# Low parts of x a group earlier, the router's small matmuls in idle bank pairs, one scaling per group

## The chip, the core and the metric

One core of a Trainium2 chip runs the whole program. The metric is the device time of one execution in microseconds (us); less is better. Five engines work side by side, each through its own instructions in order: TensorE (PE; its weight loads are PEld), VectorE (DVE), ScalarE (ACT), GpSimd (POOL) and SyncE (SP), which here issues the DMAs. SBUF is the on-chip memory, PSUM the memory that TensorE writes its sums into: eight banks, `bank[:, 0..7, :]`.

## What is computed

```python
# attention: p packs k, v into 32 rows per head; q attends to the packed rows   -> x (2304, 512)
h = x @ w_in;  x = (h * cos(h)) @ w_out                                         # first layer
logits = x @ w_gate;  P = exp(logits - logits.max())                            # router, 8 experts
for _ in range(8):
    P /= P.sum(1, keepdims=True) + 1e-09
    P /= P.sum(0, keepdims=True) + 1e-09
    P *= N / E
for e in range(E):                                                              # second layer
    out += P[:, e:e + 1] * (np.maximum(x @ w1[e], 0.0) @ w2[e])                  # 512 -> 1024 -> 512
```

Everything is fp32. A matrix that TensorE reads is split into a high part (fp32r) and a low part (the rest), and a product is three matmuls: high x high, high x low, low x high.

## The kernel before

The first part of the program (attention and first layer) is not touched. The diff lies in the second layer and its entry. The second layer has 16 units (an expert's half each) of three blocks of 768 tokens, which makes 48 **steps**. This text numbers them from 0, as the code's `now` does. A product of 2 x 2 blocks is computed with seven multiplications instead of eight, for x times w1 (`g1_mult`, products 0, 6, 1, 5, 4, 3, 2 of x) and for h times w2 (`g2_mult`, products 1, 5, 6, 3, 7, 2, 4 of h). One product is 12 matmuls of 128x384. The w2 products of a step are computed during the next step.

**A step is four groups**, k = 0 to 3. Group 0 has x's products 0 and 6, then h's products 1 and 5; group 1 has 1 and 5, then 6 and 3; group 2 has 4 and 3, then 7 and 2; group 3, half as long, has 2, then 4. So 24 or 12 matmuls stand in each half of a group. `between` is called after the first x product, and further work is recorded around the parts. The order in which the program is written is the order on each engine; nothing rearranges it.

**PSUM pairs.** x's products go into two pairs of banks, X = `two_banks(x)` and Y (banks 0 to 3), which change roles from step to step; h's products go into two pairs out of banks 4 to 7 (chain 0 and chain 1), which also change roles. X of a step is Y of the step before. A group reads them with ScalarE (L787 copy, L790 copy with a minus sign, L797 copy, L772 relu) and VectorE (L791, L805 add into PSUM); L857 (VectorE) adds a finished h product into the output `acc`, and L859 (ScalarE) writes it where it is the first. Line 746 makes the low half of an h operand behind ScalarE's cast of line 741; L812, L817, L821 are sums of h blocks on VectorE and L813 one on GpSimd.

**x.** During the first unit (steps 0 to 2) the 21 x operands are made: `x_sum` (L652, VectorE), `x_high` (L665, ScalarE cast) and `x_low` (L670, VectorE, followed by two DMAs that store the operand to DRAM, L672), into one of four slots. From the second unit on they are loaded back (L682). Before, `x_steps(n)` does one of each in the same place: low of n-2, high of n-1, sum of n, so that the low part of an operand is written three products ahead of its use.

**Router.** `logits` (32-column matmuls, transposes, `lg_sum`) runs through step 0 and `sinkhorn` behind it, as generators that `step_side` advances by one piece at fixed places. `sinkhorn` takes the maximum (`mx`, a transpose, `top`, ones x top, `nmx`), the exp on ScalarE, then eight rounds of row sums (`rs`) and column sums (`cs`, ones x cs, `rc`), and at the end transposes the probabilities to `p_sb` and stores them to `pd` in DRAM. Its small matmuls need a bank: before, that is bank 2(1-x) for the first two and bank 7 for all others; to keep bank 7 free, steps 3, 4 and 5 are **narrow**: chain 1 has only bank 6, its products are done bank by bank (`NARROW`) and each half is added on its own.

**Scaling.** The first expert's output is scaled by its column of P after the fact: `pb_load` broadcasts a block's probabilities from `pd`, and `scale_first` (L894, VectorE) multiplies one of four pieces of a block in `acc`. Before, these are steps 6, 7, 8, with one, one and two pieces in groups 0, 1 and 2. From the second expert on L775 applies the scale to the relu's result.

The other queues: SP issues all these DMAs in program order; `t_make` and `w1_make` prepare the next unit's weights on ScalarE and GpSimd (L242, L243, L246; L710, L711, L714).

## Time and profile before

| What | us |
|---|---|
| Median of three runs | 1847.51 (1846.35 to 1849.91) |
| The profiled execution, its time | 1848.91 |
| The profiled execution, its span | 1846.6 |
| TensorE busy, of that | 1814.5 |
| VectorE busy | 1479.4 |
| ScalarE, GpSimd busy | 828.2, 831.4 |
| Mean granted TensorE clock | 0.997 of full speed |

The span is the time from the first to the last instruction. The granted clock is the share of TensorE's full clock (2.4 GHz) that it was given: 1.00, or 0.50 (1.2 GHz). "Idle before" in a row is the time in which the engine had nothing to run, and the arrow names what ended it. A busy time can be longer than the work: VectorE's passes of 128x768 last about 0.95 us in most rows, and about 2 us in some.

### The profile page before, as it was taken

To read this page: it belongs to the slowest core of one execution; us is meant where nothing else is said; L and a number is where in the kernel's file an instruction comes from. 1 tells how busy PE (TensorE), PEld (TensorE's weight loads), DVE (VectorE), ACT (ScalarE), POOL (GpSimd) and SP (SyncE) were. 2 spreads that over 40 slices of the span, in tenths; PEclk is the share of its full clock that TensorE was granted. 3 is DMA by queue.
4 is the path that set the end of the run, shared out by engine and by line. 5 is a ranking of instruction groups with operands and counts; after the bars stand their busy time and mean duration, and the time that the engine had idled before them with its cause. 6 is when DMAs were issued, how large, how long until landed. Compare 5 with 4: busy or idle time off the path is not lost.

```text
span 1846.6 us, 29714 instructions
## 1 busy us (share of the span) xinstructions
PE 1814.5 (98%) x11751; PEld 1770.5 (96%) x11751; DVE 1479.4 (80%) x1613; ACT 828.2 (45%) x1243; POOL 831.4 (45%) x542
## 2 busy tenths in 40 slices
PE   7999999998999999999999999999999999999998
PEld 4799999988999999999999999999999999999998
DVE  5876877557697998888888888888788888888886
ACT  5877777655644333333333333333333333333333
POOL 3545554554343545454545444444444544544420
PEclk9999999999999999999999999999999999999999
DMA  8511111035657666666766666666666666666652
GB/s 294 182 47 46 47 58 58 1 133 189 220 194 234 224 221 218 229 211 211 229 219 211 213 229 218 211 223 220 235 210 230 222 211 219 212 228 220 212 190 108
DMA packets 220982, 345.58 MB, mean 187 GB/s; under 512 B 13852, under 2 KB 190764, under 8 KB 220844
## 3 DMA queue, kind: packets, MB, share of 16 engines
q1 hardware_dynamic: 220844, 343.68, 56.2%
q8 instruction: 93, 1.52, 0.3%
q14 instruction: 45, 0.37, 0.1%
HBM read 322.32 MB, written 21.31 MB: 186 GB/s over the span
## 4 chain that ended last, share of the span: by engine, by line
PE 89%; DVE 6%; ACT 2%; issue 1%; DMA 1%; POOL 1%; SPq 0%; ACTq 0%; DVEq 0%; POOLq 0%
PE bank L763 35%; PE bank L837 35%; PE bank L606 11%; PE bank L547 2%; PE bank L549 2%; PE bank L548 2%; DVE hreg L746 1%; DVE acc L857 1%; DMA k<-kT 1%; PE bank L483 1%; DMA pb<-pd 0%; DVE slot L746 0%; DVE xl L670 0%; PE bank L899 0%; ACT raw L772 0%
## 5 line engine op out<-in xcount | busy, mean ns | idle before, releaser
L837 PE MATMUL bank<-hreg,thi 128*128 128x384 f32 x2016 | 516.4, 337 | 2.8 <-DVE acc L857 2.0
L763 PE MATMUL bank<-xh 128*128 128x384 f32 x1344 | 454.4, 338 | 4.8 <-DVE top L948 3.4
L763 PE MATMUL bank<-xl,xh 128*128 128x384 f32 x1344 | 452.5, 337 | 1.8 <-DVE xl L670 1.8
L763 PE MATMUL bank<-xh,xl 128*128 128x384 f32 x1344 | 452.3, 336 | 0.0
L857 DVE TENSOR_TENSOR acc<-bank,acc 128x768 f32<-128x768 f32 (+1 forms) x343 | 313.4, 916 | 113.1 <-PE bank L837 110.7
L837 PEld LDWEIGHTS bank<-hreg,thi 128*128 128x128 f32 x2016 | 365.1, 188 | 4.6 <-ACT thi L242 1.3
L746 DVE TENSOR_TENSOR hreg<-raw,hreg 128x768 fp32r<-128x768 f32 x252 | 332.2, 1326 | 22.6 <-ACT hreg L741 22.5
L837 PE MATMUL bank<-hreg,tlo 128*128 128x384 f32 x1008 | 339.3, 337 | 0.0
L741 ACT CAST hreg<-raw 128x768 fp32r<-128x768 f32 x252 | 207.2, 835 | 278.6 <-DVE raw L821 134.5
L243 POOL TENSOR_TENSOR tlo<-raw,thi 128x512 fp32r<-128x512 f32 x112 | 168.0, 1505 | 260.7 <-ACT thi L242 254.9
L813 POOL TENSOR_TENSOR raw<-raw,raw 128x768 f32<-128x768 f32 x48 | 89.3, 1861 | 395.4 <-DVE raw L812 395.4
L763 PEld LDWEIGHTS bank<-xh 128*128 128x128 f32 x1344 | 253.0, 188 | 7.0 <-DVE top L948 3.8
L763 PEld LDWEIGHTS bank<-xl,xh 128*128 128x128 f32 x1344 | 253.5, 189 | 2.4 <-DVE xl L670 2.4
L763 PEld LDWEIGHTS bank<-xh,xl 128*128 128x128 f32 x1344 | 253.2, 188 | 0.0
L711 POOL TENSOR_TENSOR xl<-wraw,xh 128x512 fp32r<-128x512 f32 x112 | 188.5, 1695 | 124.3 <-ACT xh L710 124.3
L837 PEld LDWEIGHTS bank<-hreg,tlo 128*128 128x128 f32 x1008 | 189.3, 188 | 0.0
L606 PE MATMUL bank<-hreg,whi 128*128 128x288 f32 x1024 | 188.1, 296 | 0.2 <-DVE rbuf L587 0.2
L775 DVE SCALAR_TENSOR_TENSOR raw<-bank,pb 128x768 f32<-128x768 f32 x168 | 160.0, 952 | 18.5 <-PE bank L763 13.8
L837 PE MATMUL bank<-slot,thi 128*128 128x384 f32 x672 | 171.6, 336 | 0.6 <-DVE acc L857 0.6
L606 PEld LDWEIGHTS bank<-hreg,whi 128*128 128x128 f32 x1024 | 153.0, 188 | 1.9 <-DVE rbuf L587 1.1
L242 ACT CAST thi<-raw 128x512 fp32r<-128x512 f32 x112 | 68.0, 619 | 157.9 <-POOL raw L246 156.5
L563 POOL TENSOR_TENSOR hreg<-rbuf,hreg 128x576 fp32r<-128x576 f32 x64 | 91.8, 1437 | 96.4 <-ACT hreg L557 86.8
(153 smaller groups left out, 2681.0 us busy)
## 6 DMA issues: line engine op xcount, KB each, us to landing
xh<-xd SPq DMA_DIRECT2D x315, 384.0 KB, 3.4
xl<-xd SPq DMA_DIRECT2D x315, 384.0 KB, 4.1
raw<-w SPq DMA_DIRECT2D x32, 512.0 KB, 6.0
wraw<-w SPq DMA_DIRECT2D x30, 512.0 KB, 6.3
pb<-pd SPq DMA_DIRECT2D x25, 384.0 KB, 5.4
raw<-w_in SPq DMA_DIRECT2D x16, 512.0 KB, 3.8
raw<-w_out SPq DMA_DIRECT2D x16, 512.0 KB, 3.7
xd<-xh SPq DMA_DIRECT2D x21, 384.0 KB, 3.1
```

The source lines that it names most:

```text
L242: nc.scalar.copy(hi, src)
L243: nc.gpsimd.tensor_tensor(out=lo, in0=src, in1=hi.bitcast(F32), op=ALU.subtract)
L563: nc.gpsimd.tensor_tensor(out=lo, in0=r, in1=hi.bitcast(F32), op=ALU.subtract)
L606: nc.tensor.matmul(ps[:, di, 0:HC], lhsT=lhsT, rhs=rhs, start=(n in (0, 6)), stop=(n in (17, 23)),)
L711: nc.gpsimd.tensor_tensor(out=lo, in0=src, in1=hi.bitcast(F32), op=ALU.subtract)
L741: nc.scalar.copy(hi, step_tiles(s)[H_SRC[m]])
L746: nc.vector.tensor_tensor(out=lo, in0=step_tiles(s)[H_SRC[m]], in1=hi.bitcast(F32), op=ALU.subtract)
L763: nc.tensor.matmul(dst, lhsT=w, rhs=t[:, k, :], start=start and k == 0 and w is a and t is th, stop=k == 1 and w is bq, skip_group_check=True,
L775: nc.vector.scalar_tensor_tensor(out=out, in0=src, scalar=0.0, in1=scale, op0=ALU.max, op1=ALU.mult)
L813: nc.gpsimd.tensor_tensor(out=r21, in0=r11, in1=r21, op=ALU.subtract)
L837: nc.tensor.matmul(dst, lhsT=w, rhs=t[:, p, :], start=start and p == 0 and w is a and t is hh, stop=p == 1 and w is bq, skip_group_check=True,
L857: nc.vector.tensor_tensor(out=dst, in0=src, in1=dst, op=ALU.add)
```

## The change

- `x_first` and `x_next` replace `x_steps`. With q the product that a place stands behind, `x_high(q+4)` is written right after that product, and `x_low(q+4)` and `x_sum(q+6)` after the next part: the low part is now written four products ahead of its use, and so is the sum.
- `sinkhorn` yields True where it next needs a bank, and `step_side(b)` goes on there only where a bank is given. It is given in step 0 (bank 7), in group 0 of step 1 (once), and from group 2 of step 2 on at three places of a step: after the first product of group 0 and of group 3 (the first bank of chain 1's pair), and after the first part of group 2 (bank 2-2x, of Y). The pieces in between are cut differently: `rc` and the multiplication that follows are now one piece with the next round's row sums.
- Steps 3 to 5 are no longer narrow.
- `SCALES` puts one piece of the first expert's scaling into a group: block 0 from group 2 of step 5, block 1 from group 3 of step 6, block 2 from group 3 of step 7. The first `pb_load` moves from group 3 to group 0 of step 5, and the other early ones move with it.

```diff
-    free = {}
+    free = {"need": False}
     def sinkhorn():
         nc.vector.tensor_reduce(mx, lg, axis=AX.XY, op=ALU.max)
-        for _ in range(4):
-            yield
-        t_ps = bank[:, free["bank"], :]
+        yield True
+        ps = bank[:, free["bank"], :]
...
+        yield False
+        yield False
+        yield True
+        ps = bank[:, free["bank"], :]
+        nc.tensor.matmul(ps[:, 0:1], lhsT=ones[0:1, :], rhs=top, start=True, stop=True)
...
             nc.vector.tensor_reduce(cs, prob.rearrange("p t e -> p e t"), axis=AX.X, op=ALU.add)
-            yield
-            yield
-            c_ps = bank[:, 7, :]
-            nc.tensor.matmul(c_ps[:, 0:E], lhsT=ones, rhs=cs, start=True, stop=True)
+            yield True
+            ps = bank[:, free["bank"], :]
+            nc.tensor.matmul(ps[:, 0:E], lhsT=ones, rhs=cs, start=True, stop=True)
...
-    def step_side():
+    def step_side(b=None):
         while side:
+            if free["need"] and b is None:
+                return
+            free["bank"] = b
...
-        def x_steps(n, tmp, end=7 * NJ):
-            if 1 < n <= end + 1 and (n > 5 or end == 4):
+        def x_first(n, tmp):
+            if 1 < n:
                 x_low(n - 2)
...
+        SCALES = {
+            divmod(at + n, 4): (i, n) for i, at in enumerate((22, 27, 31)) for n in range(4)
+        }
-                narrow = s in (NJ * U1 + 3, NJ * U1 + 4, NJ * U1 + 5, NJ * NU - 1)
+                narrow = s == NJ * NU - 1
...
+                    def side_at(place):
+                        if now == 0:
+                            step_side(7)
+                        elif now > 2 or now == 2 and k > 1 or (now, k, place) == (1, 0, 1):
+                            step_side({
+                                (0, 1): banks[1][0], (2, 2): 2 - 2 * x, (3, 1): banks[1][0],
+                            }.get((k, place)))
...
-                        if 2 * NJ <= now < 3 * NJ:
-                            for n in ((0,), (1,), (2, 3), ())[k]:
-                                scale_first(now - 2 * NJ, n, pb[(2, 2, 0)[now - 2 * NJ]])
-                        if busy or k == 3:
-                            free["bank"] = 2 * (1 - x)
-                            step_side()
+                        if (now, k) in SCALES:
+                            scale_first(*SCALES[now, k], pb[2 if now < 7 or now == 7 and k < 3 else 0])
+                        side_at(1)
+                        if qs:
+                            x_next(x_high, qs[0] + 4)
...
-                            if first_unit and 2 * k + n < 7 and 7 * j + 2 * k + n + 3 < 7 * NJ + 2:
-                                x_steps(7 * j + 2 * k + n + 5, [halves(t) for t in pb])
+                            side_at(2 + n)
+                            if n == 0 and len(qs) > 1:
+                                x_next(x_high, qs[1] + 4)
+                            if n < len(qs):
+                                x_next(x_low, qs[n] + 4)
+                                x_next(x_sum, qs[n] + 6, tmp)
...
-                        (5, 3, 1, 0, 0), (5, 3, 0, 0, 2), (5, 3, 1, 1, 1), (6, 2, 0, 1, 2),
+                        (5, 0, 0, 0, 2), (5, 2, 1, 0, 0), (5, 2, 1, 1, 1), (6, 1, 0, 1, 2),
```

Three places show what this does to the engines' order. The first is ScalarE at the turn from step 0 to step 1: L772 relu of group 3, then `x_high` (L665), weight and h casts, and group 0's two copies (L787 and L790). Before:

```order
L772 ACTIVATE raw_4410<-bank 128x768
L665 CAST xh<-pb_3998 128x2x384
L242 CAST thi<-raw_4059 128x512
L741 CAST hreg<-raw_4411 128x768
L787 COPY raw_4001<-bank 128x768
L790 ACTIVATE base<-bank 128x768
L859 COPY acc_101<-bank 128x2x384
```

The same place after the change:

```order
L741 CAST hreg<-raw_4411 128x768
L787 COPY raw_4001<-bank 128x768
L955 ACT_TABLE_LOAD
L955 ACTIVATE prob<-lg,nmx 128x144
L665 CAST xh<-pb_3997 128x2x384
L790 ACTIVATE base<-bank 128x768
L859 COPY acc_101<-bank 128x2x384
```

The router's exp with its table load, which stood in step 2's group 3, and a cast of x now stand between the two copies of group 0.

The second is VectorE from there into group 1: L805 of step 0's group 3, low parts (L670) and sums (L652) of x, h splits (L746) and sums (L817, L821), L791 of group 0. Before:

```order
L805 TENSOR_TENSOR bank<-bank,base 128x2x384
L670 TENSOR_TENSOR xl<-acc_101,xh 128x2x384
L746 TENSOR_TENSOR hreg<-raw_4411,hreg 128x768
L817 TENSOR_TENSOR raw_4411<-raw_4411,raw_4408 128x768
L791 TENSOR_TENSOR bank<-bank,raw_4001 128x2x384
L746 TENSOR_TENSOR hreg<-raw_4411,hreg 128x768
L670 TENSOR_TENSOR xl<-pb_3998,xh 128x2x384
L652 TENSOR_TENSOR pb_3998<-acc_101,pb_3998 128x768
L670 TENSOR_TENSOR xl<-pb_3997,xh 128x2x384
L821 TENSOR_TENSOR raw_4411<-raw_4410,raw_4411 128x768
```

After the change, from the pass behind L805 on:

```order
L947 TENSOR_REDUCE top<-bank 1x1
L670 TENSOR_TENSOR xl<-pb_3998,xh 128x2x384
L652 TENSOR_TENSOR pb_3998<-acc_101,pb_3998 128x768
L746 TENSOR_TENSOR hreg<-raw_4411,hreg 128x768
L817 TENSOR_TENSOR raw_4411<-raw_4411,raw_4408 128x768
L954 COPY nmx<-bank 128x1
L791 TENSOR_TENSOR bank<-bank,raw_4001 128x2x384
L746 TENSOR_TENSOR hreg<-raw_4411,hreg 128x768
L670 TENSOR_TENSOR xl<-pb_3997,xh 128x2x384
L670 TENSOR_TENSOR xl<-pb_3998,xh 128x2x384
L652 TENSOR_TENSOR pb_3997<-acc_1628 128x768
L821 TENSOR_TENSOR raw_4411<-raw_4410,raw_4411 128x768
```

`top` and `nmx`, which stood in steps 1 and 2, stand here now, and one more sum of x lies ahead of the first L746.

The third is VectorE in groups 2 and 3 of step 2: two adds L857 and a split L746 before, and L805 of group 3. Before:

```order
L812 TENSOR_TENSOR raw_4411<-raw_4409,raw_4000 128x768
L857 TENSOR_TENSOR acc_101<-bank,acc_101 128x2x384
L746 TENSOR_TENSOR hreg<-raw_4408,hreg 128x768
L857 TENSOR_TENSOR acc_1628<-bank,acc_1628 128x2x384
L805 TENSOR_TENSOR bank<-bank,base 128x2x384
L953 COPY nmx<-bank 128x1
```

After the change, from the first of those adds on:

```order
L857 TENSOR_TENSOR acc_101<-bank,acc_101 128x2x384
L746 TENSOR_TENSOR hreg<-raw_4408,hreg 128x768
L972 TENSOR_SCALAR rc<-bank 128x8
L973 RECIPROCAL rc<-rc 128x8
L974 SCALAR_TENSOR_TENSOR prob<-prob,rc 128x144
L959 TENSOR_REDUCE rs<-prob 128x18
L960 TENSOR_SCALAR rs<-rs 128x18
L961 RECIPROCAL rs<-rs 128x18
L857 TENSOR_TENSOR acc_1628<-bank,acc_1628 128x2x384
L963 TENSOR_TENSOR prob<-prob,rs 128x144
L967 TENSOR_REDUCE cs<-prob 128x8
L805 TENSOR_TENSOR bank<-bank,base 128x2x384
```

A round of the router now lies between the split and L805, and its `cs` is what the small matmul of group 3 reads.

## Rows read from the trace of the kernel before

**Rows 1.** The page, part 1: busy time, share of the span, instructions.

```profile
PE 1814.5 (98%) x11751; PEld 1770.5 (96%) x11751; DVE 1479.4 (80%) x1613; ACT 828.2 (45%) x1243; POOL 831.4 (45%) x542
```

**Rows 2.** Busy time by stretch: steps 1, 2, 3, 4, 6, 8.

```profile
419.06:454.05 34.99, 30.35 (x172) 29.17 (x170) 29.21 (x30) 20.49 (x29) 14.74 (x10) 0.98 0.60 205
454.05:488.34 34.29, 32.71 (x170) 32.13 (x171) 22.85 (x22) 20.90 (x30) 14.97 (x10) 0.92 0.56 182
488.34:522.09 33.75, 31.23 (x177) 30.12 (x177) 27.08 (x47) 17.65 (x28) 13.29 (x9) 1.00 0.64 210
522.09:554.10 32.01, 30.75 (x178) 30.12 (x178) 29.93 (x56) 13.20 (x19) 10.21 (x7) 1.00 0.62 206
...
583.77:614.99 31.22, 30.24 (x170) 29.20 (x169) 25.64 (x25) 9.09 (x13) 11.23 (x7) 1.00 0.78 255
...
644.68:674.00 29.32, 29.32 (x169) 29.32 (x169) 28.95 (x26) 10.46 (x15) 16.62 (x11) 1.00 0.62 200
```

**Rows 3.** TensorE's waits over the whole span: total us, times, longest.

```profile
PE bank L763 <- DVE top L948: 3.4, 1, 3.4
PE bank L837 <- DVE acc L857: 2.6, 5, 1.3
PE bank L763 <- DVE xl L670: 1.8, 2, 1.6
PE bank L970 <- DVE cs L966: 1.2, 2, 0.6
PE bank L763 <- ACT raw L772: 1.0, 1, 1.0
```

**Rows 4.** Stretches around two waits (columns as Rows 2), then the chain.

```profile
475.50:477.42 1.92, 0.34 (x3) 0.02 (x2) 1.92 (x2) 1.74 (x3) 1.92 (x2) 1.00 0.03 10
...
452.82:454.05 1.23, 0.00 (x1) 0.00 (x1) 1.23 (x4) 0.21 (x1) 1.23 (x1) 0.50 0.98 361
...
454.05 6.96 PE bank L763 x24
```

**Rows 5.** Timeline of ScalarE: start, duration, line; steps 1 and 2.

```profile
424.91 0.82 ACT L790 ACTIVATE base<-bank 128x768 f32<-128x768 f32 x1
...
487.76 1.28 ACT L954 ACT_TABLE_LOAD   x1
489.05 0.42 ACT L954 ACTIVATE prob<-lg,nmx 128x144 f32<-128x144 f32 x1
```

**Rows 6.** Timeline of VectorE, groups 0 and 1 of step 1.

```profile
425.80 1.93 DVE L817 TENSOR_TENSOR raw<-raw,raw 128x768 f32<-128x768 f32 x1
427.66 0.95 DVE L791 TENSOR_TENSOR bank<-bank,raw 128x768 f32<-128x768 f32 x1
...
434.10 1.07 DVE L746 TENSOR_TENSOR hreg<-raw,hreg 128x768 fp32r<-128x768 f32 x1 [0.90 <-ACT hreg L741]
```

**Rows 7.** Timeline of VectorE, end of step 1.

```profile
450.92 2.01 DVE L652 TENSOR_TENSOR pb<-acc,pb 128x768 f32<-128x768 f32 x1
452.86 0.95 DVE L805 TENSOR_TENSOR bank<-bank,base 128x768 f32<-128x768 f32 x1
```

**Rows 8.** Timelines of GpSimd and VectorE, group 2 of step 3.

```profile
514.09 1.83 POOL L813 TENSOR_TENSOR raw<-raw,raw 128x768 f32<-128x768 f32 x1 [2.46 <-DVE raw L812]
...
514.39 2.33 DVE L746 TENSOR_TENSOR hreg<-raw,hreg 128x768 fp32r<-128x768 f32 x1
```

**Rows 9.** Timeline of VectorE: router passes of step 3.

```profile
493.13 0.45 DVE L966 TENSOR_REDUCE cs<-prob 128x8 f32<-128x144 f32 x1
...
497.27 0.16 DVE L972 TENSOR_SCALAR rc<-bank 128x8 f32<-128x8 f32 x1
...
499.23 0.27 DVE L960 RECIPROCAL rs<-rs 128x18 f32<-128x18 f32 x1
```

**Rows 10.** Timelines of SP and VectorE: the loads of pb and the first scaling.

```profile
583.40 1.78 SPq L886 DMA_DIRECT2D pb<-pd  x3
...
592.06 1.69 DVE L894 TENSOR_TENSOR acc<-acc,pb 128x768 f32<-128x768 f32 x1 [5.28 <-DMA pb<-pd]
```

More of the change, by code (lines that the diff above doesn't have):

```diff
@@ L942, in sinkhorn @@
         nc.vector.tensor_reduce(mx, lg, axis=AX.XY, op=ALU.max)
-        for _ in range(4):
-            yield
-        t_ps = bank[:, free["bank"], :]
-        nc.tensor.transpose(t_ps[0:1, 0:P], mx, ident)
+        yield True
+        ps = bank[:, free["bank"], :]
+        nc.tensor.transpose(ps[0:1, 0:P], mx, ident)
         top = small.tile([1, 1], F32, tag="top", name="top")
-        nc.vector.tensor_reduce(top, t_ps[0:1, 0:P], axis=AX.X, op=ALU.max, negate=True)
-        yield
-        b_ps = bank[:, free["bank"], :]
-        nc.tensor.matmul(b_ps[:, 0:1], lhsT=ones[0:1, :], rhs=top, start=True, stop=True)
+        nc.vector.tensor_reduce(top, ps[0:1, 0:P], axis=AX.X, op=ALU.max, negate=True)
+        yield False
+        yield False
+        yield True
+        ps = bank[:, free["bank"], :]
+        nc.tensor.matmul(ps[:, 0:1], lhsT=ones[0:1, :], rhs=top, start=True, stop=True)
         nmx = small.tile([P, 1], F32, tag="nmx", name="nmx")
-        nc.vector.tensor_copy(nmx, b_ps[:, 0:1])
+        nc.vector.tensor_copy(nmx, ps[:, 0:1])
         nc.scalar.activation(prob, lg, AF.Exp, bias=nmx, scale=1.0)
-        yield
+        yield False
         for k in range(8):
@@ L980, in sinkhorn @@
         nc.vector.tensor_copy(by_e, prob.rearrange("p t e -> p e t"))
-        yield
-        yield
-        t_ps = bank[:, 7, :]
+        yield True
+        ps = bank[:, free["bank"], :]
         half = E // 2 * NT // P
@@ L986, in sinkhorn @@
             nc.tensor.transpose(
-                t_ps[0:half, P * i:P * i + P],
+                ps[0:half, P * i:P * i + P],
                 by_e[:, E // 2 * i:E // 2 * i + E // 2, :].rearrange("p e t -> p (e t)"), ident,
             )
-        nc.scalar.copy(p_sb[0:half, :], t_ps[0:half, 0:2 * P])
+        nc.scalar.copy(p_sb[0:half, :], ps[0:half, 0:2 * P])
         nc.sync.dma_start(
@@ L993, in sinkhorn @@
         )
-        yield
     side = []
-    def step_side():
+    def step_side(b=None):
         while side:
+            if free["need"] and b is None:
+                return
+            free["bank"] = b
             try:
-                next(side[0])
+                free["need"] = next(side[0])
                 return
@@ L1004, in step_side @@
                 side.pop(0)
+                free["need"] = False
     with tc.manual_schedule():
@@ L1170, in tile_kernel @@
             if s >= n0 + 10:
-                x_steps(s - n0 - 10, [halves(t) for t in pb], 4)
+                x_first(s - n0 - 10, [halves(t) for t in pb])
             if n0 + 8 <= s < n0 + 12:
@@ L1206, in tile_kernel @@
                     now = s - NJ * U1
-                    busy = now == 0 or now >= NJ
+                    tmp = [halves(t) for t in pb]
+                    qs = [7 * j + n for n in range(2 * k, min(2 * k + 2, 7))] if first_unit else []
+                    def side_at(place):
[5 more added lines that the diff above has]
+                            }.get((k, place)))
                     def between():
@@ L1211, in between @@
                             h_low(s - 1, 3)
-                        if 2 * NJ <= now < 3 * NJ:
-                            for n in ((0,), (1,), (2, 3), ())[k]:
-                                scale_first(now - 2 * NJ, n, pb[(2, 2, 0)[now - 2 * NJ]])
-                        if busy or k == 3:
-                            free["bank"] = 2 * (1 - x)
-                            step_side()
-                    if busy:
-                        step_side()
+                        if (now, k) in SCALES:
[3 more added lines that the diff above has]
+                            x_next(x_high, qs[0] + 4)
+                    side_at(0)
+                    if now == 0 and k == 0:
+                        x_sum(5, tmp)
                     if prev is not None:
```

16 lines of the change are left out of this document (7 added, 9 removed).

## The prediction

> **What bounds the kernel now.** I read the page first: TensorE is busy for 98% of the span [rows 1], so time can only be won where it stands or runs slowly. I then cut the stretch that the diff touches into steps, each beginning at the first matmul of its product 0. Step 8, which the diff does not disturb, takes 29.32 us for its 169 matmuls; it is the clean step. Steps 1, 2, 3, 4, 6 take 34.99, 34.29, 33.75, 32.01 and 31.22 us [rows 2], that is 5.67, 4.97, 4.43, 2.69 and 1.90 us too much, together 19.7 us; steps 5 and 7 have little and are left alone. That is all that this change can touch. Who is waited for stands in the table of TensorE's waits [rows 3]: 3.4 us for `top`, 2.6 us for the adds into `acc` (the narrow steps), 1.8 us for the low parts of x, 1.2 us for `cs`, 1.0 us for a relu on ScalarE. To the wait for `top` belongs what followed it: the granted clock was 0.50 from 452.82 us on, and the 24 matmuls after the wait took 6.96 us [rows 4]. At the clean step's pace (29.32/169 = 0.1735 us) 24 matmuls take 4.16 us, so the low level (half, 1.2 GHz) cost 2.8 us. A wait of 1.92 us in step 2 kept the granted clock at 1.00 [rows 4].
>
> **Step 1: the exp comes forward.** Removed: the wait for `top` (3.4 us), since its transpose now goes into bank 7 a step earlier, and the waits for xl and for the relu shrink. Added: ones x top in group 0 of step 1, and behind it `nmx` on VectorE and the exp on ScalarE. The table load (1.28 us) waits for nothing, but the exp waits for `nmx`, and `nmx` stands behind the sum of line 817, which ran from 425.80 to 427.73 us [rows 5, 6]. Queued behind the exp on ScalarE are a cast of x, the copy of line 790 and an evacuation, and VectorE's L791 waits for line 790. From the rows: 427.73 + 0.15 (nmx, as the 0.16 of line 972 [rows 9]) + 0.42 (exp) + 2 x 0.8 (the cast, as line 790, and line 790 itself, 0.82) = 429.9 us, where L791 began at 427.66 us before [rows 5, 6]: 2.2 us later. Between L791 and the L746 of 434.10 us stand as many passes as before (one split, two low parts, one sum, L821, and a cast on ScalarE), so that L746 ends 2.2 us later as well, at 437.4 instead of 435.2 us, and the matmuls of h's product 3 had begun right at its end. TensorE stood some 1.3 us in that part of step 1 before; it now stands 3.5 us, spread over two or three waits (the second pair's first product must also wait until `nmx` is read). With 0.15 us for the small matmul the excess of step 1 is 3.7 us, a gain of 2.0. Bounds: L817 lasted 1.93 us where its neighbour L791 lasted 0.95, and if it is not stretched this time, 1.0 less (2.7); if a later pass is stretched likewise, 1.0 more (4.7).
>
> **Step 2: what comes last without top.** Product 6 of step 2 writes the pair that L805 and the relu behind it still read. VectorE is late there: it began L805 at 452.86 us, right at the end of the sum of x before it (450.92 + 2.01) and with no idle time [rows 7]. Of its queue ahead of L805 the change takes one sum of x (line 652, 2.01 us beside a GpSimd pass, some 0.95 without [rows 7]); so L805 comes about 1.1 us earlier, and with it (0.95) and a relu (0.8, as line 790) the pair is free at about 453.6 us on the old scale, while TensorE, without the wait, is there at 454.05 - 3.4 + 12 x 0.1735 - 0.4 (the wait for xl that goes) = 452.3. A wait of 1.3 us remains (0.3 if the sum that goes was worth its 2.0 us, 2.3 if nothing comes earlier), too short to take the clock down if the rows of 1.92 us are a guide. Then a low part and a sum of x now stand ahead of the split that product 5 needs: 1.0 us (0 to 1.9). The 1.6 us wait for xl of group 2 [rows 3] goes: that low part now has a whole group. The router starts here: small matmuls in groups 2 and 3, 0.15 us each, and a wait, next. Excess 1.3 + 1.0 + 0.3 (small gaps, as before) + 1.6 + 0.45 = 4.65 us against 4.97, a gain of 0.3; bounds 1.5 and 7.5.
>
> **The router's waits (steps 2 to 4).** Each step now has three small matmuls, at fixed places: after x's product 0 in group 0, between h's two parts in group 2, and after x's product 2 in group 3. The last of them follows its predecessor by two blocks of 12 matmuls, 4.2 us. In between VectorE must do, in order: the split L746, which begins beside GpSimd's L813 and is held until that ends (514.39 us, 2.33 us, against GpSimd's 1.83 us from 514.09 [rows 8]); the six passes from line 972 to 960 (497.27 to 499.50: 2.2 us with one of them stretched, 1.6 without [rows 9]); one add (0.9); and two passes for `cs` (0.8, of which 0.45 is line 966 [rows 9]). Counted from the start of group 2: the r21 relu is done at 5.1, L812 at 6.0, L813 and the held split at 8.75, then 10.3 to 10.9, 11.2 to 11.8, `cs` at 12.0 to 12.6 us; TensorE is there at 10.7 us (five blocks of 2.1 and a small matmul). A wait of 1.6 us (0.4 if the split is not held, 2.6 if another GpSimd pass intervenes) in each of steps 2, 3 and 4. The other two places have 4 us or more of room. The narrow steps' half adds go (2.6 us of waits, and about one add's time of work per step), as do the old waits for `cs`. Excess of steps 3 and 4: 1.6 + 0.45 = 2.1 us each; gains 2.3 and 0.6.
>
> **The scaling (steps 5 to 8).** Before, VectorE stood 5.28 us for the first `pb`, issued at 583.40 us in a batch of three and used at 592.06 [rows 10], and then had twelve scalings to catch up with. Now p is stored and the first load issued a step earlier, in group 0 of step 5, behind one pair of x loads on SP's queue; 8.7 us from issue to use, the row's time for three transfers, still end before the first scaling two groups (16 us) later. One scaling (0.95 to 1.7 us) stands in each group, two of them in step 5, where VectorE no longer has the router. The wait goes with what followed it: gain 1.9 us, step 6's excess. What hides the scalings is VectorE's spare time: it was busy for 25.6 of step 6's 31.22 us and 29.0 of step 8's 29.32 [rows 2], the latter with the four scalings of block 2 in it and no wait that shows; if that does not suffice, half the excess stays and the gain is 1.0.
>
> **The sum.** 2.0 + 0.3 + 2.3 + 0.6 + 1.9 = 7.1 us off the profiled execution's own 1848.91 us (its span is 1846.6): 1841.8. That execution lay 1.4 us above the median of 1847.51 us, so the forecast for a median is 1840.4, rounded 1840.5 us. The bounds, all on one side at once, move the gain between 0.3 and 13.7 us: 1833.8 to 1847.2.
>
> **Rivals.** (a) The clock falls once in one of the new waits, most likely that of step 1 or of a group 3. Rows: it fell in a wait of 3.4 us and held in one of 1.92 us [rows 3, 4]; mine are 1.3 to 2.6 us. Price 2.8 us and the longer wait itself, 0.9: 1844.1 us, within 0.2% of before. The Trainium skill ("TensorE: Matmul & The Clock Gate", What's actually happening) says that the check behind the gate runs freely, so that the moment of a change differs from run to run; by it no length between the two rows is safe and a run that is caught comes to 1844.1 us, while by the rows alone waits up to 1.9 us are safe and the sum stays. No run here shows waits in between. I follow the rows for the forecast and give this rival its chance for the waits near 2.5 us.
> (b) Slower: in group 3 of each of steps 2, 3 and 4 VectorE is another GpSimd pass later (t_make and w1_make run there; 1.8 us, as L813), the wait is 2.6 us and the clock falls each time: 3 x (1.0 + 2.8) = 11.4 us on the forecast, 1851.9 us. It decides from waits of about 2.4 us on. For it: VectorE was at 30 of 32 us in step 4 [rows 2]; against: the half adds are gone from there.
> (c) The exp's path is hidden and VectorE reaches `cs` in time: step 1 keeps 1.3 us (2.4 less), the router 0.4 in each step (3.6 less), and product 5 of step 2 waits for nothing (1.0 less): 1833.5 us.
> (d) The low parts, though earlier in the order, are not earlier in time, since VectorE is late from step 1 on; the wait of group 2 in step 2 then stays (1.6): 1842.1 us.
>
> **How the numbers follow.** Forecast 0.46, (a) 0.26, (b) 0.10, (c) 0.12, (d) 0.06. A measurement of this kernel can tell about 0.2% (3.7 us): faster is below 1843.8 us, slower above 1851.2. Of the forecast's range the last 3.4 us lie above 1843.8 (0.40 of 0.46 below it), (c) lies below (0.12), (d) mostly (0.05), (a) in its better part (0.05): 0.62. Slower is (b), 0.10; the rest, 0.28, is no difference. The range goes from 1834.0, which leaves out half of (c) at most, to 1847.5, past the bounds and past (a) with a second long wait; (b) is left out.
>
> **What would show it.** In the changed kernel's trace: no wait for `top`; granted clock 1.00 through steps 1 to 4 (otherwise (a) or (b)); a standing TensorE of 2 to 4 us in groups 0 and 1 of step 1 behind line 790 or L746; about 1.3 us before product 6 of step 2; waits for `cs` near 1.6 us in group 3 of three steps and none elsewhere; no VectorE wait for `pb`; step 6 at 29.3 us. I am wrong if step 1 comes out clean or near 36 us, or if steps 3 and 4 are not near 31.4 us.

## The result: 0.7% slower

| What | before | after |
|---|---|---|
| Median of four runs, us | 1847.29 (1846.35 to 1849.91) | 1860.47 (1859.54 to 1861.67) |
| Ratio, with its 95% interval | | 1.0069 (1.0052 to 1.0087) |
| The profiled execution: its time, span, us | 1848.91, 1846.6 | 1859.54, 1857.5 |
| Mean granted clock | 0.997 | 0.992 |

The change costs about 13 us where a gain of 7 was forecast. The profiled executions differ by 10.9 us of span, and that difference lies in a few steps. These are the stretches of steps 0 to 4, 6 and 8 after the change (columns as in [rows 2]; the column behind the POOL figures is the granted clock):

```profile
386.23:421.78 35.55, 33.36 (x219) 28.27 (x216) 20.72 (x26) 16.80 (x27) 19.82 (x12) 0.95 0.40 145
...
421.78:455.93 34.15, 32.03 (x172) 31.16 (x171) 26.48 (x27) 21.77 (x30) 8.89 (x7) 0.95 0.46 154
455.93:494.83 38.90, 33.38 (x174) 31.63 (x173) 31.81 (x44) 20.22 (x29) 21.22 (x12) 0.92 0.64 224
494.83:532.45 37.62, 32.97 (x176) 32.33 (x175) 22.82 (x39) 16.56 (x23) 14.30 (x9) 0.91 0.45 147
532.45:567.00 34.55, 32.00 (x175) 31.68 (x175) 24.45 (x38) 14.36 (x20) 12.36 (x9) 0.94 0.58 190
596.79:626.14 29.35, 29.35 (x170) 29.35 (x169) 25.83 (x25) 9.83 (x15) 12.74 (x8) 1.00 0.71 236
655.46:684.78 29.32, 29.32 (x170) 29.32 (x169) 28.33 (x27) 10.58 (x15) 17.14 (x10) 1.00 0.63 203
```

Step 0 of the kernel before, which the prediction did not look at, is this stretch of its trace:

```profile
386.97:419.06 32.09, 31.91 (x218) 26.86 (x215) 18.55 (x25) 17.02 (x27) 16.50 (x11) 1.00 0.36 128
```

Step by step, after less before: 0: +3.5; 1: -0.8; 2: +4.6; 3: +3.9; 4: +2.5; 6: -1.9 us. TensorE's waits in steps 0 to 8 of the changed kernel (total us, times, longest) name the cause; beside [rows 3], `top`, xl and the adds L857 are gone, and `cs` has taken their place (L970 is the router's small matmul, ones x `cs`; L763 and L837 are the products of x and h):

```profile
PE bank L970 <- DVE cs L967: 10.5, 4, 4.2
PE bank L925 <- DVE acc L617: 2.2, 1, 2.2
PE bank L837 <- DVE nmx L954: 1.8, 1, 1.8
PE bank L763 <- ACT raw L772: 1.1, 1, 1.1
PE bank L837 <- DVE hreg L746: 1.0, 2, 0.7
```

To each of the long ones belongs a stretch at half the clock. These five windows of the changed kernel are all that is granted 0.50 between 380 and 640 us (before, one such stretch of 6.83 us, see [rows 4]); in the order of the fence they begin inside or right behind the waits of group 3 in steps 2, 3 and 4, the one of step 0 and the one of step 1:

```profile
488.95:495.78 6.83, 5.38 (x17) 5.39 (x18) 4.27 (x12) 1.52 (x3) 0.00 (x0) 0.50 0.68 245
526.50:533.33 6.83, 5.32 (x17) 5.32 (x18) 4.34 (x12) 1.45 (x2) 0.85 (x1) 0.50 0.13 48
564.05:567.46 3.41, 3.41 (x13) 3.41 (x12) 1.09 (x6) 2.05 (x3) 1.97 (x2) 0.50 0.06 20
417.27:420.68 3.41, 3.41 (x14) 3.12 (x13) 1.75 (x5) 1.00 (x2) 2.07 (x2) 0.50 0.08 30
430.92:434.33 3.41, 3.41 (x12) 3.41 (x12) 1.43 (x2) 3.41 (x6) 0.00 (x0) 0.50 0.32 115
```

**Group 3 of step 2.** The chain of waits of the changed kernel there (start, us, what) runs through VectorE and reaches TensorE only with the small matmul L970:

```profile
484.83 1.87 DVE hreg L746
...
487.05 0.98 DVE prob L974
...
488.87 0.81 DVE acc L857
...
489.93 0.42 DVE cs L967
...
490.39 0.60 PE bank L970 x2
```

TensorE had waited 3.35 us when L970 began (4.22 us in step 3 and 2.55 in step 4), so it was there at 487.04. VectorE had no idle time between 476.03 us and the end of `cs` (490.34). VectorE's timeline of the changed kernel in group 2 of step 2 (start, duration), and GpSimd's beside it, show why it was late:

```profile
477.78 2.07 DVE L670 TENSOR_TENSOR xl<-acc,xh 128x768 fp32r<-128x768 f32 x1
...
480.64 0.28 DVE L959 TENSOR_REDUCE rs<-prob 128x18 f32<-128x144 f32 x1
...
483.01 0.95 DVE L812 TENSOR_TENSOR raw<-raw,raw 128x768 f32<-128x768 f32 x1
483.88 0.95 DVE L857 TENSOR_TENSOR acc<-bank,acc 128x768 f32<-128x768 f32 x1
484.75 1.95 DVE L746 TENSOR_TENSOR hreg<-raw,hreg 128x768 fp32r<-128x768 f32 x1
...
487.05 0.97 DVE L974 SCALAR_TENSOR_TENSOR prob<-prob,rc 128x144 f32<-128x144 f32 x1
...
484.04 1.85 POOL L813 TENSOR_TENSOR raw<-raw,raw 128x768 f32<-128x768 f32 x1 [3.02 <-DVE raw L812]
485.85 2.02 POOL L711 TENSOR_TENSOR xl<-wraw,xh 128x512 fp32r<-128x512 f32 x1
```

The low part of x (2.07 us) and the router's first round (from 480.64 to 482.2) stand ahead of L812; behind it L746, which starts beside GpSimd's L813, takes 1.95 us and ends 0.8 us after that one (485.89), and the small pass L974, 0.31 us where GpSimd is idle, takes 0.97 beside L711. In step 3 the queue starts late because of ScalarE, whose cast for L746 stood behind a weight cast (L242) that waited for GpSimd, and three small passes are held (one line of ScalarE's timeline, then VectorE's):

```profile
516.27 0.62 ACT L242 CAST thi<-raw 128x512 fp32r<-128x512 f32 x1 [3.15 <-POOL raw L246]
...
518.36 0.96 DVE L746 TENSOR_TENSOR slot<-raw,slot 128x768 fp32r<-128x768 f32 x1 [3.77 <-ACT slot L741]
...
523.29 0.96 DVE L974 SCALAR_TENSOR_TENSOR prob<-prob,rc 128x144 f32<-128x144 f32 x1
...
524.61 0.78 DVE L960 TENSOR_SCALAR rs<-rs 128x18 f32<-128x18 f32 x1
...
526.42 1.09 DVE L963 TENSOR_TENSOR prob<-prob,rs 128x144 f32<-128x144 f32 x1
```

**Step 0.** A sum for x (L652) now stands ahead of L617, the last add of the first layer, which the router's matmuls L925 read; the sum lasts 2.56 us beside GpSimd's L813, where 0.95 is its length with GpSimd idle. Timelines of VectorE, GpSimd and TensorE:

```profile
413.32 2.56 DVE L652 TENSOR_TENSOR pb<-acc,pb 128x768 f32<-128x768 f32 x1
415.81 0.74 DVE L617 SCALAR_TENSOR_TENSOR acc<-bank,acc 128x576 f32<-128x576 f32 x1
...
412.62 2.46 POOL L813 TENSOR_TENSOR raw<-raw,raw 128x768 f32<-128x768 f32 x1 [2.30 <-DVE raw L812]
...
416.61 0.88 PE L925 MATMUL bank<-acc,wgs 128*32 128x384 f32 x4 [2.19 <-DVE acc L617]
```

**Step 1.** `nmx` frees the bank that h's product 5 needs (VectorE, then TensorE):

```profile
430.38 0.15 DVE L954 COPY nmx<-bank 128x1 f32<-128x1 f32 x1
...
430.68 0.76 PE L837 MATMUL bank<-hreg,thi 128*128 128x384 f32 x2 [1.83 <-DVE nmx L954]
```

### The profile page after: what moved, and what is told of

Same layout as the page of the kernel before. It is cut to its first block, busy times and chain, and to the rows that moved or that the text cites. A ratio compares the mean times of both kernels' runs of the same rounds, so it can differ in the third digit from the quotient of the medians.

```text
span 1857.5 us, 29699 instructions
## 1 busy us (share of the span) xinstructions
PE 1818.4 (98%) x11751; PEld 1777.2 (96%) x11751; DVE 1476.5 (79%) x1600; ACT 827.6 (45%) x1241; POOL 836.9 (45%) x542
## 4 chain that ended last, share of the span: by engine, by line
PE 72%; DVE 2%; ACT 0%; issue 0%; POOL 0%; ACTq 0%; DVEq 0%; POOLq 0%
PE bank L837 36%; PE bank L763 35%; DVE acc L857 0%; PE bank L899 0%; DVE xl L670 0%; DVE slot L746 0%; DVE hreg L746 0%; POOL tlo L243 0%; POOL raw L246 0%; DVE prob L974 0%; DVE raw L821 0%; DVE rs L960 0%; DVE prob L963 0%; DVE raw L817 0%; PE bank L970 0%
## 5 line engine op out<-in xcount | busy, mean ns | idle before, releaser
L837 PE MATMUL bank<-hreg,thi 128*128 128x384 f32 x2016 | 519.7, 338 | 3.0 <-DVE nmx L954 1.8
L763 PE MATMUL bank<-xh 128*128 128x384 f32 x1344 | 453.7, 338 | 1.1 <-ACT raw L772 1.1
L763 PE MATMUL bank<-xl,xh 128*128 128x384 f32 x1344 | 451.8, 336 | 0.0
L763 PE MATMUL bank<-xh,xl 128*128 128x384 f32 x1344 | 451.8, 336 | 0.0
L857 DVE TENSOR_TENSOR acc<-bank,acc 128x768 f32<-128x768 f32 (+1 forms) x330 | 309.7, 939 | 119.8 <-PE bank L837 117.6
L837 PEld LDWEIGHTS bank<-hreg,thi 128*128 128x128 f32 x2016 | 368.0, 189 | 4.3 <-issue 2.1
L746 DVE TENSOR_TENSOR hreg<-raw,hreg 128x768 fp32r<-128x768 f32 x252 | 334.2, 1333 | 26.6 <-ACT hreg L741 26.5
L837 PE MATMUL bank<-hreg,tlo 128*128 128x384 f32 x1008 | 341.1, 338 | 0.0
L813 POOL TENSOR_TENSOR raw<-raw,raw 128x768 f32<-128x768 f32 x48 | 89.4, 1863 | 397.7 <-DVE raw L812 397.7
L763 PEld LDWEIGHTS bank<-xh 128*128 128x128 f32 x1344 | 253.3, 188 | 2.2 <-ACT raw L772 1.4
L763 PEld LDWEIGHTS bank<-xl,xh 128*128 128x128 f32 x1344 | 253.2, 188 | 0.0
L763 PEld LDWEIGHTS bank<-xh,xl 128*128 128x128 f32 x1344 | 252.9, 188 | 0.0
L711 POOL TENSOR_TENSOR xl<-wraw,xh 128x512 fp32r<-128x512 f32 x112 | 190.4, 1712 | 121.7 <-ACT xh L710 121.7
L837 PEld LDWEIGHTS bank<-hreg,tlo 128*128 128x128 f32 x1008 | 190.8, 189 | 0.0
L837 PE MATMUL bank<-slot,thi 128*128 128x384 f32 x672 | 173.4, 339 | 0.0
L242 ACT CAST thi<-raw 128x512 fp32r<-128x512 f32 x112 | 68.1, 619 | 155.6 <-POOL raw L246 154.2
```

The costliest lines, as they stand in the source:

```text
L242: nc.scalar.copy(hi, src)
L711: nc.gpsimd.tensor_tensor(out=lo, in0=src, in1=hi.bitcast(F32), op=ALU.subtract)
L746: nc.vector.tensor_tensor(out=lo, in0=step_tiles(s)[H_SRC[m]], in1=hi.bitcast(F32), op=ALU.subtract)
L763: nc.tensor.matmul(dst, lhsT=w, rhs=t[:, k, :], start=start and k == 0 and w is a and t is th, stop=k == 1 and w is bq, skip_group_check=True,
L813: nc.gpsimd.tensor_tensor(out=r21, in0=r11, in1=r21, op=ALU.subtract)
L837: nc.tensor.matmul(dst, lhsT=w, rhs=t[:, p, :], start=start and p == 0 and w is a and t is hh, stop=p == 1 and w is bq, skip_group_check=True,
```

## The experiments

The theory from these rows: the router's matmul of group 3 comes too soon for VectorE, whose passes are held by GpSimd, and each wait takes the clock down; step 0 and step 1 add one wait each. The rivals: (A) the x part makes VectorE late and the router only shows it; (B) VectorE's chain is late as such, and any other deadline shows the same. Ratios are to the kernel before, run on the same chip, with 95% intervals. The steps are from each profiled execution; step 0 begins there at 386.2 to 389.5 us, so the steps do not add up to the differences of the medians. Of the kernels changed from after, only "in another bank", "split late" and "all four" have intervals that lie wholly below that of after; the effect of each other edit is read from waits and steps, not from the median:

| Kernel | Median us | Ratio | Step 0 | 1 | 2 | 3 | 4 | 6 |
|---|---|---|---|---|---|---|---|---|
| before | 1847.3 | | 32.1 | 35.0 | 34.3 | 33.8 | 32.0 | 31.2 |
| after | 1860.5 | 1.0069 | 35.6 | 34.2 | 38.9 | 37.6 | 34.6 | 29.4 |
| x part alone | 1849.5 | 1.0004 (0.9994 to 1.0013) | 35.6 | 34.7 | 30.0 | 33.8 | 32.1 | 31.2 |
| x and scaling | 1846.4 | 0.9988 (0.9978 to 0.9997) | 35.8 | 34.8 | 30.0 | 33.7 | 32.0 | 29.3 |
| router alone | 1859.6 | 1.0060 (1.0043 to 1.0077) | 32.2 | 32.9 | 40.1 | 37.9 | 34.5 | 31.4 |
| after, L970 of group 3 without cs | 1856.4 | 1.0043 (1.0028 to 1.0058) | 35.6 | 34.2 | 36.6 | 35.7 | 32.8 | 29.4 |
| the same, in another bank | 1854.7 | 1.0035 (1.0021 to 1.0048) | 35.9 | 34.1 | 33.3 | 33.2 | 36.2 | 29.4 |
| after, no L813 in steps 2 to 4 | 1855.6 | 1.0041 (1.0027 to 1.0055) | 35.6 | 34.2 | 36.7 | 35.4 | 33.3 | 29.3 |
| after, exp in group 2 | 1857.7 | 1.0052 (1.0037 to 1.0067) | 35.9 | 32.3 | 37.6 | 37.7 | 34.5 | 29.4 |
| after, rounds spaced | 1853.7 | 1.0039 (1.0024 to 1.0053) | 35.6 | 32.8 | 34.6 | 34.8 | 33.7 | 29.3 |
| after, split late | 1855.6 | 1.0034 (1.0021 to 1.0047) | 35.9 | 34.1 | 37.0 | 34.1 | 33.3 | 29.4 |
| after, sum late | 1857.2 | 1.0050 (1.0035 to 1.0065) | 33.3 | 34.0 | 37.7 | 38.1 | 34.6 | 29.3 |
| all four together | 1841.8 | 0.9967 (0.9955 to 0.9980) | 33.3 | 32.2 | 33.0 | 30.7 | 31.9 | 29.3 |
| x and scaling, sum late | 1844.6 | 0.9981 (0.9972 to 0.9990) | 32.2 | 35.6 | 30.0 | 33.8 | 32.0 | 29.4 |

### Which part loses

The change was cut into its parts. The x part alone is the diff's `x_first` and `x_next` and their calls in the kernel before:

```diff
-                                x_steps(7 * j + 2 * k + n + 5, [halves(t) for t in pb])
+                                x_next(x_low, qs[n] + 4)
+                                x_next(x_sum, qs[n] + 6, tmp)
```

> The kernel before with only the x part of the change (high and low parts of x a group earlier, the temporary tiles as in the changed kernel); router, narrow steps and scaling as before. Theory (the loss sits in the router's third small matmul of steps 2 to 4, and a smaller part in step 0, where a sum for x now stands ahead of the L617 add): step 0 about 3.5 us longer, as in the changed kernel, the waits for xl (1.8 us) gone, nothing lost in steps 2 to 4; 1849 us (1847 to 1851). Rival A (the earlier x parts load VectorE so that whatever follows is late): steps 1 and 2 longer too, 1853 us or more.

The second adds the scaling (`SCALES` and the earlier loads of pb), the router as before:

```diff
+                        if (now, k) in SCALES:
+                            scale_first(*SCALES[now, k], pb[2 if now < 7 or now == 7 and k < 3 else 0])
```

> The kernel before with the x part and the scaling part of the change, the router as before. Theory: the one with the x part alone less the 1.90 us of step 6 and about 0.4 of step 7, so 1846.5 us (1845 to 1849), below or at the kernel before. Rival A: 1851 us or more.

The third has the router part alone (the new `sinkhorn`, `step_side` and `side_at`, no narrow step but the last):

```diff
-                narrow = s in (NJ * U1 + 3, NJ * U1 + 4, NJ * U1 + 5, NJ * NU - 1)
+                narrow = s == NJ * NU - 1
```

> The kernel before with the router part alone (small matmuls in the banks that lie idle, no step narrow but the last); x and scaling as before. Theory: this part carries the loss. Steps 2 to 4 show the same waits for cs in group 3 (2.7 to 4.4 us each, with the clock at half after each), step 0 as before, step 1 without the wait for top: 1857 us (1853 to 1862). Rival A (the x part makes VectorE late, and the router only shows it): waits for cs under 1.6 us each, 1845 us.

All three came out as the theory has it: 1849.5, 1846.4 and 1859.6 us. The x part wins 4.3 us in step 2 (34.3 to 30.0) and loses 3.5 in step 0. Of the 4.3, some 2.8 are what the half-clock matmuls behind the wait for `top` cost in before: that wait, 3.44 us there, is 2.76 us here, and the clock stayed at 1.00 in this execution. The other 1.6 are the wait for xl; the scaling brings step 6 from 31.2 to 29.3. The router alone shows the same waits as the whole change, here TensorE's row of it:

```profile
PE bank L970 <- DVE cs L967: 10.1, 3, 4.2
```

Rival A falls: without the x part the waits are 3.33, 4.24 and 2.55 us, against 3.35, 4.22 and 2.55 with it. Medians of parts do not quite add up (-1.7 and +11.5 make +9.8 us, the whole is +13.2, each against runs of before beside it); the wait for `nmx` in step 1 is 1.06 us with the router alone, with the clock at 1.00, and costs the clock only with x and router together.

### What is late: cs, the bank, or VectorE

First the operand was taken away: the matmul of group 3 multiplies a constant tile.

```diff
-            nc.tensor.matmul(ps[:, 0:E], lhsT=ones, rhs=cs, start=True, stop=True)
+            nc.tensor.matmul(ps[:, 0:E], lhsT=ones, rhs=ones[:, 0:E] if free["blind"] else cs, start=True, stop=True)
...
+                        free["blind"] = now and (k, place) == (3, 1)
```

> The changed kernel, but the small matmul of group 3 (steps 2 to 4) multiplies with a constant tile instead of cs, so that TensorE has nothing to wait for there; the router's weights, and with them the output, are not the reference's. All else is issued as it was. Theory: the three waits (3.5, 4.4 and 2.7 us) go, and with them the half-clock stretches behind them (17 us at half the clock, 8.5 us lost): 1841.5 us (1839 to 1845). Rival B (the chain on VectorE is late as such, and its lateness comes out at the next small matmul, in group 0 of the following step, or at the products' operands): two thirds or more of it comes back, 1852 us or more.

1856.4 us: the theory in this form falls (the waits did not go: they are 2.67, 2.78 and 1.74 us and have changed their name). TensorE's waits in that run:

```profile
PE bank L970 <- DVE acc L857: 7.2, 3, 2.8
...
PE bank L970 <- DVE cs L967: 0.4, 1, 0.4
```

The bank is not idle in group 3: the second chain's add L857, which reads it, stands on VectorE behind the router's own passes (488.87 in the chain above) and ends 0.65 to 1.45 us ahead of `cs`. So the bank was taken away too:

```diff
-                                (0, 1): banks[1][0], (2, 2): 2 - 2 * x, (3, 1): banks[1][0],
+                                (0, 1): banks[1][0], (2, 2): 2 - 2 * x, (3, 1): 3 - 2 * x,
```

> The changed kernel with the small matmul of group 3 (steps 2 to 4) not only multiplying a constant tile instead of cs, but also written to the second bank of the product pair that lies idle there, instead of the second chain's bank; output not the reference's. In the run with the constant tile alone TensorE waited at the same three places for the second chain's add L857, which VectorE makes behind the router's chain. Theory: cs and that add are two deadlines missed for one reason, VectorE's late chain, and with both out of the way the group 3 waits (2.8, 2.9 and 1.9 us there) and the half-clock stretch behind them go: 1843 us (1840 to 1847). Rival (the lateness then comes out at the next router matmul or at the products): 1852 us or more.

1854.7 us, the rival's number. No wait stands in group 3 any more. TensorE waits instead right behind it, for the reading of that bank (`rc`) at the next step's product 0 and for `cs` at the next router matmul, and of steps 2 to 4 the clock fell in the last (0.91 there):

```profile
PE bank L763 <- DVE rc L972: 3.0, 3, 1.8
PE bank L970 <- DVE cs L967: 2.3, 3, 1.0
```

So rival B holds: what is late is VectorE's queue from group 2 on, and a deadline taken away shows the next one. Only a part of the price goes with each (-4.1 and -1.7 us; the intervals of the two runs overlap), as the next deadline lies a little later. GpSimd's part in it was measured by leaving L813 out in steps 2 to 4:

```diff
-        nc.gpsimd.tensor_tensor(out=r21, in0=r11, in1=r21, op=ALU.subtract)
+        if not 2 <= NJ * (u - U1) + j <= 4:
+            nc.gpsimd.tensor_tensor(out=r21, in0=r11, in1=r21, op=ALU.subtract)
```

> The changed kernel without the GpSimd pass L813 (r21 = r11 - r21) in steps 2 to 4, so that the products that use it get other numbers and the output is not the reference's. Theory: the VectorE pass L746 beside it falls from 1.95 us to 0.95 and cs comes 1.0 us earlier: waits of 2.5, 3.4 and 1.7 us, half-clock stretches there fewer by one or none: 1856.5 us (1853.5 to 1859). Rival (the next GpSimd pass in line, of w1's or w2's preparation, takes its place beside VectorE): 1859 us or more.

1855.6 us, inside the theory's range, but the rival has a part in it: other GpSimd passes now stand beside VectorE. In step 2 the split and the small pass behind it are back at their own length, while another split ahead of them is held (beside GpSimd's L711); in step 3 the split takes 1.49 us and the small pass 0.97, and in step 4 they take 1.28 and 0.97 (VectorE's timeline of that run, whose lines are numbered one higher from L813 on; steps 2 and 3):

```profile
483.43 2.04 DVE L746 TENSOR_TENSOR hreg<-raw,hreg 128x768 fp32r<-128x768 f32 x1
...
487.13 0.94 DVE L746 TENSOR_TENSOR hreg<-raw,hreg 128x768 fp32r<-128x768 f32 x1
...
488.43 0.31 DVE L975 SCALAR_TENSOR_TENSOR prob<-prob,rc 128x144 f32<-128x144 f32 x1
...
521.08 0.97 DVE L975 SCALAR_TENSOR_TENSOR prob<-prob,rc 128x144 f32<-128x144 f32 x1
```

The waits fell from 3.35, 4.22 and 2.55 to 2.79, 2.49 and 2.14 us. L813 is thus worth 0.4 to 1.7 us of each wait. What all of GpSimd's holds are worth no run shows. An estimate from the rows of the changed kernel: the held passes of VectorE ahead of `cs` (L670, L746 and L974 in step 2; L746, L974, L960 and L963 in steps 3 and 4) last 2.8, 3.1 and 2.1 us longer than with GpSimd idle, so that they could make up most of the waits if nothing else came last; the prediction had allowed some 2 us of it per step. The Trainium skill ("SBUF — State Buffer", SBUF: two separate sides) says that a GpSimd instruction that reads SBUF and a VectorE one with two SBUF inputs exclude each other for the whole instruction; the rows agree (L746 1.95 with, 0.94 without L813, while L857, one of whose inputs is in PSUM, takes 0.95 beside L813).

### Single repairs

The exp's broadcast two groups later:

```diff
-                        elif now > 2 or now == 2 and k > 1 or (now, k, place) == (1, 0, 1):
+                        elif now > 2 or now == 2 and k > 1 or (now, k, place) == (1, 2, 2):
```

> The changed kernel with the broadcast of top (and with it nmx and the exp) two groups later, in group 2 of step 1, in the pair that lies idle there. Theory: TensorE's wait for nmx in group 0 of step 1 (1.8 us by the waits, a gap of 1.99) and the half-clock stretch behind it (3.4 us, 1.7 lost) go: 1857 us (1855 to 1859.5). Rival: the wait moves with the exp to group 2 and VectorE's products behind it come late there: 1860 us.

1857.7 us: the wait for `nmx` is gone and step 1 is at 32.3 us with the clock at 1.00. The rounds further apart, and the one small matmul of group 0 in step 1 behind that group's first part:

```diff
-                        elif now > 2 or now == 2 and k > 1 or (now, k, place) == (1, 0, 1):
+                        elif now > 2 or now == 2 and k > 1 or (now, k, place) == (1, 0, 2):
...
-                                (0, 1): banks[1][0], (2, 2): 2 - 2 * x, (3, 1): banks[1][0],
+                                (0, 2): banks[1][1], (2, 2): 2 - 2 * x, (3, 2): banks[1][0],
```

> The changed kernel with the three rounds of a step further apart: the third matmul after the part of group 3 instead of before it, the first of the next step after the first part of group 0 instead of before it (in the second bank of the idle pair); so 6.3, 6.3 and 16.8 us of products between them, where the changed kernel has 4.2, 4.2 and 21. Theory: each wait in group 3 falls by 2.1 us (3.5, 4.4, 2.7 to 1.4, 2.3, 0.6), the wait for the bank's add goes altogether, and one or two of the five half-clock stretches are left there: 1849 us (1845 to 1854). Rival (VectorE has too much to do in the narrow place whatever the spacing, and the new places make the next part wait for the bank): 1857 us or more.

1853.7 us, the upper end of the expectation. The waits of group 3 fell to 1.26, 2.15 and 0.48 us, 2.1 us each, and no half-clock stretch is left in steps 1 to 4 of the profiled execution. That was the fastest of five, 1852.0 us at a mean clock of 0.997; the slowest took 1855.9 us at 0.993, so the clock fell for longer there. At the new place in group 0 the next part waits for `rc`, as the rival had it (TensorE's waits):

```profile
PE bank L970 <- DVE cs L967: 4.3, 4, 2.2
PE bank L837 <- DVE rc L972: 4.0, 2, 2.6
```

The split of the next operand out of VectorE's way:

```diff
-                                elif k == 2:
+                                elif k == (3 if 2 <= now <= 4 else 2):
                                     split_h(s, 1)
```

> The changed kernel with the split of the next part's operand in steps 2 to 4 (a copy on ScalarE and a VectorE pass of 1.95 us, held by the GpSimd pass of first_sums) taken out of group 2 and issued after group 3's part, so that it no longer stands ahead of the router's chain. Theory: cs and the bank's add are ready 1.7 to 1.9 us earlier in each of steps 2 to 4, waits of about 1.7, 2.6 and 0.9 us are left, and one or two half-clock stretches go: 1852 us (1848 to 1856). Rival (the chain is late because it starts late, whatever stands in it): 1858 us or more.

1855.6 us, near the upper end of the range: group 3 waits 2.05, 1.55 and 0.51 us, but the next round, in group 0, now waits too (1.24 and 2.33 us), since the moved split stands ahead of it (in step 3 that split itself waits 3.4 us for ScalarE's cast). The sum for x of step 0 behind L617:

```diff
-                                x_next(x_sum, qs[n] + 6, tmp)
+                                late = now == 0 and k == 2
+                                for q in qs[n * (not late):(n + 1) * (n or not late)]:
+                                    x_next(x_sum, q + 6, tmp)
```

> The changed kernel with the one sum for x that stands ahead of the add L617 in group 2 of step 0 issued behind it. Theory: the router's matmuls L925 no longer wait 2.2 us for that add, and the half-clock stretch behind (3.4 us, 1.7 lost, of which some may be granted elsewhere) goes; step 0 takes 32.1 us as in the kernel before: 1857 us (1855.5 to 1859). Rival (GpSimd's pass holds the add itself, whatever stands ahead): 1859.5 us or more.

1857.2 us: step 0 falls from 35.6 to 33.3 us, with the clock at 1.00; of the remaining 1.2 us against before, 0.9 are a wait for `mx` at the turn to step 1, which now shows.

### A version that beats both

> The changed kernel with the single changes together: the exp in group 2 of step 1, the rounds 6.3 us apart, the sum for x of step 0 behind the add L617, and the operand split of steps 2 to 4 issued at the end of group 3, behind the router's chain; besides, the round in group 0 stands ahead of the split of the second operand, since in the run with the rounds apart the next part waited there for rc (1.6 and 2.8 us). Theory: step 0 at 32.1 us, step 1 at about 31.5, no wait over 1 us for cs, the bank or rc in steps 2 to 4, and no half-clock stretch behind them; what stays are the waits for r12 (1.3 us) and for parts of h (0.9 and less) in step 2: 1836 us (1833 to 1841), below both kernels. Rival (the gains overlap, or the split issued late makes the next step's first part wait): 1844 us or more.

The edit is the four above, with the split at the very end of group 3 and `side_at(2)` of group 0 ahead of `split_h(s - 1, 6)`. 1841.8 us, 0.33% faster than before and, by the medians, 1.0% faster than after; 0.8 us above the expected range. The stretches of steps 0 to 4:

```profile
388.19:421.49 33.30, 32.19 (x220) 26.82 (x216) 20.94 (x27) 16.79 (x27) 19.74 (x12) 1.00 0.43 155
421.49:453.67 32.18, 30.63 (x172) 29.58 (x173) 26.80 (x28) 21.79 (x30) 9.82 (x7) 1.00 0.50 171
453.67:486.71 33.04, 31.20 (x173) 29.48 (x173) 27.52 (x34) 18.67 (x27) 20.21 (x12) 1.00 0.61 208
486.71:517.41 30.70, 30.28 (x177) 29.96 (x176) 21.14 (x40) 16.34 (x23) 12.57 (x9) 1.00 0.64 213
517.41:549.31 31.90, 30.24 (x177) 29.93 (x176) 25.74 (x43) 13.53 (x19) 11.27 (x8) 1.00 0.64 205
```

The clock is at 1.00 in all of them. The expectation of no wait over 1 us missed one, 1.7 us for `rc` in group 0 of step 4, and steps 0 and 1 took 33.3 and 32.2 us where 32.1 and 31.5 were expected (0.9 us is the wait for `mx`). What the repaired router part is worth was asked last, with the router as before and the late sum:

> The kernel before with the x part and the scaling part, and the sum for x of step 0 behind the add L617; the router as before. It tells what the router part is worth once its waits are repaired. If the repaired router (all single changes together, 1841.8 us) is worth something, this one lies above it: by the steps of the run with x and scaling, less the 2.3 us that the late sum gave in step 0, 1844 us (1842 to 1846). If the router part is worth nothing even then, 1841 us or less.

1844.6 us, as expected. The repaired router part is thus worth some 2.8 us (1841.8 against 1844.6; measured on different chips, and the ratios' intervals overlap, so its size is not firm): it wins 3.4 and 3.1 us in steps 1 and 3 and gives 3.0 and 1.1 back in steps 2 and 0. The clock alone can do as much: of the fifteen runs of before beside this kernel one, at a mean clock of 1.000, took 1841.6 us, and the others 1846.5 to 1851.1 us at 0.995 to 0.999.

## Why the prediction was wrong

Right were the steps on x and the scaling. The waits for `top`, xl and the narrow steps' adds went; the wait for product 6 in step 2 came to 1.1 us (1.3 forecast), L791 of step 1 came 2.1 us later into its step (2.2 forecast: 10.67 against 8.60 us from the step's start), step 6 fell to 29.35 us and no load of pb is waited for.

**The failing step is "The router's waits (steps 2 to 4)".** Its 1.6 us per step, at most 2.6, measured 3.35, 4.22 and 2.55. Its count took VectorE as free when the r21 relu ends, with L812 done at 6.0 us, the held split at 8.75, `cs` at 12.0 to 12.6 and TensorE there at 10.7. On that scale, with TensorE's arrival as 10.7, step 2 had L812 done at 7.6 (the low part of x and the first round stood ahead), the split at 10.4, `cs` at 14.0. Step 3 had them at 7.1 (a late cast on ScalarE), 9.8 and 14.9, since three of the small passes were held by GpSimd where the estimate had allowed one. In step 4 the first two came as counted (6.0 and 8.8), and `cs` at 13.2, with two small passes held for long and one a little. The bank's release by L857 was not counted at all, though it would alone have cost 2.67, 2.78 and 1.74 us, as the run without `cs` shows.

Part of this stood in the trace of before. Group 2 of its step 3, the step of [rows 8], begins at 505.72 us, and VectorE's timeline has

```profile
513.06 0.95 DVE L812 TENSOR_TENSOR raw<-raw,raw 128x768 f32<-128x768 f32 x1
```

so L812 was done 8.3 us after the start of the group, and the held split of [rows 8] 11.0 us, both 2.3 us later than the count.

**The clock.** Rival (b) came nearest, with a VectorE later than counted, waits of 2.6 us, a clock that falls in each and a price of 3 x 3.8 = 11.4 us; its point against ("the half adds are gone from there") was wrong, because VectorE's share of a whole step says nothing of the 10 us ahead of one deadline. Steps 2, 3 and 4 together cost 11.0 us more than before and 14.3 more than forecast (33.97, 31.42 and 31.42 us). Of the 14.3, 5.3 us are the longer waits and some 7 us the clock, half of the 14.1 us that TensorE was busy in the three half-clock stretches there (an estimate from the windows above). The row that the prediction took for a safe wait of 1.92 us [rows 4] holds 0.34 us of matmuls: the wait in it was 1.58 us.

**Two terms were left out.** Step 0 was assumed untouched: 3.5 us, from one sum that the earlier x parts put ahead of L617. In step 1 the wait for `nmx` was foreseen, but not that the clock falls in it: 34.15 us against 33.0 forecast. The later L746 that was to make TensorE stand 3.5 us cost it 0.29 us at h's product 3; it stood some 2.1 us in that step, 1.83 of them for `nmx`. Less standing and a fallen clock are misses of opposite sign, so it is in part luck that step 1 is only 1.1 us off. Both terms stand in the order of the instructions on VectorE, where step 0 was not read.

The errors add up: 3.46 (step 0) + 1.13 (step 1) + 14.26 (steps 2 to 4) is 18.85 us, less 0.74 by which step 0 began earlier in the profiled execution of after: 18.1, where forecast and measured execution differ by 17.7 (1841.8 and 1859.54).

## What to carry to other kernels

A small matmul put between large ones is a deadline for the engine that makes its operand and for the one that frees its bank: count that engine's whole queue from the last place where it was seen idle, with each pass that GpSimd can hold at its held length, before trusting a gap of some us, and compare the count with the rows at the same place of the kernel before. Put such rounds as far apart as the idle banks allow; 2.1 us more room took 2.1 us off each wait, and in the profiled execution the clock's falls in steps 2 to 4 went with them. When an operand's production is moved earlier, read what it now stands ahead of in every step, the first one included.
